# A Fourier-mixing and cosine-gated feed-forward kernel: one batch's transform work three steps later, one table load moved, another PSUM bank for the special offsets

## The chip, the cores and the metric

One NeuronCore of one Trainium2 chip runs the kernel, which works in float32 throughout. The metric is the device time of one execution in microseconds (us), the median of several runs. The profile is of one further execution.

## The reference

```python
X = np.fft.fft(x, axis=1)            # x: (8, 3008, 256)
X = np.fft.fft(X, axis=2)
x = X.real.reshape(24064, 256)
h = x @ w_in                         # (256, 2048)
g = h * np.cos(h)
out = g @ w_out                      # (2048, 256)
```

## The kernel before, in words

**The transform.** The DFT along the last axis is folded into the first weight: `WC` and `WS` are the cosine and sine tables times `w_in`. The DFT along the sequence, 3008 = 47 x 64, is done in two stages for each of the 8 batches. In the first stage rows of x are loaded into tiles `xp` (four for a batch, p = 0 to 3), GpSimd (POOL) folds each of them (`fold_x`, L376), TensorE (PE) multiplies the folded tile by the table `L2` (`pair_half`, L399), ScalarE (ACT) copies the result out of PSUM (`keep_z`, L410), POOL folds it again (`fold_z`, L417), and DMAs write it to a scratch tensor `zd` in DRAM (`store_pair`, L485). `load_z` (L495) reads `zd` back in another layout, one DMA pair for each half of the partitions. In the second stage (`second_half`, L509) PE multiplies that by the table `BJ`, one group g of 6 at a time.

Offsets 0 and 32 of the 64, and column 128, do not fit the folding and are done apart. Their rows of x are loaded into `xz` at the end of `load_xx(b, 0)` (L216), `fold_ends` (L390 on POOL, and a small ACT copy at L287 that waits in the list `small` for the next half step) folds them, `take_middle` (L369) collects column 128 of each `xp`, and once in a batch `middle` (L447) multiplies both into one PSUM tile `pm`. VectorE (DVE) clears `pm` first (`clear_middle`, L433), and ACT copies it to `zm` afterwards (L1067).

**The main part.** A step is one batch, one group g and one of 8 parts fp of the hidden width: 8 x 6 x 8 = 384 steps. Group 0 has T = 225 columns, the others 256. A step has two halves, u = 0 and 1, and the loop over k (L1022) runs through the halves, with t = k // 2 the step. For one half: ACT writes the seed of a PSUM bank (`seed`, L680), PE adds the `WC` product and then the `WS` product (`mm1`, L699), between them ACT copies out twice the first sum (`act_e`, L711), DVE forms the mirrored half of the columns (`dve_h`, L715), ACT rounds (L727), DVE takes the fraction (L731), ACT takes the sine (L737), and DVE multiplies (`dve_g`, L741). POOL forms sums of the four quarters of a step (`sums`, L757, L763, L764), and seven products with w_out and its combinations go into the accumulators `M` (`mm2`, L790), five halves later. Results leave by `take_m`, `combine_m`, a transpose on DVE (`store_out`, L910) and output DMAs (`send_out`, L928).

**Order.** All engines work through their instructions in the order of the program, and the order is written out by hand. The four banks `H0` to `H3` of the halves go round: `psum("H")` takes the next bank, and `borrow(name, k)` takes the bank that the k-th next half will get. Thus `borrow` with k = 0 is the bank of the half that is three halves back, and with k = 1 that of the half two back, which is `old` in the loop and which `dve_g(old)` reads.

While the steps of batch b run, the work of batch b + 1 is done between them. `transform(b)` (L547) makes a table from step number within the batch (0 to 47) to calls; at the end of step t the loop makes the calls that stand under t % 48. Before this table's calls of a step come those of `opening`, a table for the first steps of all. The pair products of tile p run at the start of step 8p + 9 (`pairs`), `middle` runs in the second half of step 10 (`middles`), the loads of `zd` are issued after steps 23 and 39, and `second_half` follows from step 42 on. Nearly all DMAs are issued by the SP queue, in the order of the program.

Batch 0 is transformed ahead of the loop, by other functions (`chunk`, `first_half`). The first batch to which `transform` applies is b = 1, whose work runs during steps 0 to 47. Just ahead of the loop the SP queue issues the rest of the loads, the last of them

```python
load_bj(1024, NJ * 128)
nc.sync.dma_start(out=L2, in_=L2_dr.ap())
```

and during steps 0 to 6 `opening` also has POOL combine parts of w_out (`combine_w2`, L665).

Of the kernel before, what the change touches and what calls it, by code (L numbers as in the profile page):

```python
# [21 lines left out]
NJ = 24  # L22
# [107 lines left out]
def kernel(  # L130
# [113 lines left out]
    def load_bj(c0, c1):  # L244
        nc.sync.dma_start(out=BJ[:, c0:c1], in_=B_dr.ap()[:, c0:c1])
# [4 lines left out]
    def load_w2(f0, f1):  # L250
        nc.sync.dma_start(
            out=w2.rearrange("p (q c) -> p q c", c=ND)[:, 2 * f0 : 2 * f1],
            in_=moe_w_out.rearrange("(q p) c -> p q c", p=128)[:, 2 * f0 : 2 * f1],
        )
# [24 lines left out]
    def borrow(name, k=0):  # L279
        return ppool.tile([128, 512], FP, tag=f"H{(turn[0] + k) % 4}", bufs=1, name=name)  # L280
# [115 lines left out]
    def pair_half(b, p, q, pz):  # L396
        rows = slice(64 * q, 64 * q + 64)
        for h in range(2):
            nc.tensor.matmul(  # L399
                pz[64 * h : 64 * h + 64],  # L400
                lhsT=L2[rows, 0:64],
                rhs=ws[b, p][rows, 512 * h : 512 * h + 512],
                start=True,
                stop=True,
            )
# [23 lines left out]
        small.append(dict(out=zv[:, 1, :, 0].rearrange("y (q s) -> y q s", s=2), in_=zq[:, p]))  # L429

    def clear_middle():
        pm = borrow("pm", 1)[:, 0:144]
        nc.vector.memset(pm, 0.0)  # L433
        return pm

# [100 lines left out]
    def spread_nb(g):  # L536
        pq, nb = ready[0, g]
        T = _width(g)
        pn = borrow("pn") if g else psum("pn", "M")
        nc.tensor.matmul(pn[:, 0:T], lhsT=ones, rhs=pq[0:1, T : 2 * T], start=True, stop=True)  # L540
        nc.scalar.copy(out=nb[:, 0:T], in_=pn[:, 0:T])

    pairs = {}
    middles = set()
    per = NG * 8

    def transform(b):  # L547
        todo = {}

        def at(o, *call):  # L550
            todo.setdefault(o, []).append(call)

        for p in range(4):
            if p < 2:
                at(p, turn_x, b, p)
            at(1 + p, load_xx, b, p)
            at(5 + p, take_middle, b, p)
            for k in range(2):
                at(8 * p + 6 + k, fold_x, b, p, k)
                at(8 * p + 9 + k, fold_z, b, p, k)  # L560
            pairs[per * (b - 1) + 8 * p + 9] = b, p
            at(8 * p + 11, patch_z, b, p)
            at(8 * p + 12, store_pair, b, p)
        for e in range(2):
            at(4 + e, fold_ends, e)
        middles.add(per * (b - 1) + 10)
        at(12, store_ends, b)
        at(23, load_z, b, 0)
        at(39, load_z, b, 1)
        for g in range(NG):  # L570
            at(42 + g, second_half, b, g)
        return todo
# [6 lines left out]
    def weights(e, n, tag="M"):  # L579
        pw = psum("pw", tag)  # L580
        for i in range(2):
            nc.tensor.matmul(
                pw,
                lhsT=CS[i][:, 128 * e : 128 * e + 128],
                rhs=raw(n, i),
                start=(i == 0),
                stop=(i == 1),
            )
        return pw
# [94 lines left out]
    def seed_first(h):  # L684
        s, T = h.s, h.s.T
        nc.tensor.matmul(
            h.H[:, 0:T],
            lhsT=wrow[:, 128 * h.u : 128 * h.u + 128],
            rhs=s.pq[0:1, T : 2 * T],
            start=False,  # L690
            stop=True,
            skip_group_check=True,
        )

    def mm1(h, e):
        s, T = h.s, h.s.T
        W = WS if e else WC
        f = 2 * s.fp + h.u
        nc.tensor.matmul(  # L699
            h.H[:, 0:T],  # L700
            lhsT=W[:, 128 * f : 128 * f + 128],
            rhs=s.pq[:, e * T : e * T + T],
            start=False,
            stop=True,
            skip_group_check=True,
        )

    def act_e(h):
        T = h.s.T
        h.ew = spool.tile([128, 256], FP, tag="ew", bufs=2, name="ew")  # L710
        nc.scalar.mul(out=h.ew[:, 0:T], in_=h.H[:, 0:T], mul=2.0)  # L711
# [11 lines left out]
    def act_round(h):  # L723
        if h.u == 0:
            h.s.r = spool.tile([128, 1024], FP, tag="r", bufs=4, name="r")
        r, y = sides(h)
        nc.scalar.activation(out=r, in_=y, func=AF.Copy, bias=BIG, scale=1.0)  # L727
# [11 lines left out]
    def dve_g(h):  # L739
        r, y = sides(h)  # L740
        nc.vector.scalar_tensor_tensor(  # L741
            out=r, in0=y, scalar=-0.25, in1=r, op0=ALU.add, op1=ALU.mult
        )
# [237 lines left out]
    for half in range(2):  # L981
        load_z(0, half, 4)
    load_w2(4, 6)
    load_w2(6, 8)
    load_bj(1024, NJ * 128)
    nc.sync.dma_start(out=L2, in_=L2_dr.ap())
    opening = {
        0: ((combine_w2, 0, 2), (combine_w2, 2, 4)),
        3: ((combine_w2, 4, 6, 0, 2),),
        4: ((combine_w2, 4, 6, 2, 4), (second_half, 0, 1)),  # L990
        5: ((combine_w2, 6, 8, 0, 2), (spread_nb, 1)),
# [15 lines left out]
    def step(t, last=None):  # L1007
        s = steps[t] if 0 <= t < n else None
        return s if s is not None and (last is None or s.fp == 7) else None
# [3 lines left out]
    def unit(k):  # L1013
        return halves[k] if 0 <= k < 2 * n else None
# [7 lines left out]
    for k in range(2 * n + LAG):  # L1022
        t, u = divmod(k, 2)
        d, v = divmod(k - LAG, 2)
        cur, prev, old, nxt = unit(k), unit(k - 1), unit(k - 2), unit(k + 1)
        done = step(d)
        full = step(d if v else d - 1, True)
        if cur:
            if k % (2 * per) == 0:
                todo = transform(cur.s.b + 1) if cur.s.b + 1 < NB else {}  # L1030
            if k >= AHEAD:
                mm1(cur, 0)
                act_e(cur)
            if k == 0:
                for h in (cur, nxt):
                    mm1(h, 0)
                    seed_first(h)
                    act_e(h)
                spread_nb(0)
            if k < AHEAD - 1:  # L1040
                mm1(cur, 1)
            if k == 0:
                pw = [weights(1, 3)]
        pair = None if u else pairs.pop(t, None)
        if old:
            dve_g(old)
            if old.u:
                sums(old.s)
        pm = clear_middle() if u and t in middles else None
        if done:  # L1050
            order = (0, 1, 5, 4, 3, 2, 6) if done is steps[-1] else range(7)
            mm2(done, 4 * v, 4 * v + (1 if pair else 3), order)
        if pair:
            pz = [borrow("pz"), borrow("pz", 1)]
            for q in range(2):
                pair_half(*pair, q, pz[q])
            mm2(done, 4 * v + 1, 4 * v + 3, order)
        if pm is not None:
            middle(pm)
        if full and full is not steps[-1]:  # L1060
            take_m(full, 1 if v else 3, nc.vector)
        if nxt and 0 < k < AHEAD - 1:
            seed(nxt)
        if prev:
            act_round(prev)
        if pm is not None:
            nc.scalar.copy(out=zm, in_=pm)  # L1067
        if pair:
            keep_z(*pair, 0, pz[0])
        if nxt and k >= AHEAD - 1:  # L1070
            seed(nxt)
        if full and full is not steps[-1]:
            take_m(full, 0 if v else 2, nc.scalar)
        if prev:
            dve_frac(prev)
        if k + 1 in range(2, AHEAD):
            mm1(nxt, 0)
            act_e(nxt)
        if k in (1, 2):
            pw.append(weights(0, 4 - k))  # L1080
        copy_small()
        if prev:
            act_sin(prev)
        if pair:
            keep_z(*pair, 1, pz[1])
        if cur and k >= AHEAD - 1:
            mm1(cur, 1)
        if done and v == 0:
            mm2(done, 3, 4, order)
        if cur:  # L1090
            dve_h(cur)
        if k in (1, 2, 3):
            e, q = ((1, 3), (0, 3), (0, 2))[k - 1]
            keep_weights(e, q, pw[k - 1], nc.vector.tensor_copy)
        if k == 3:
            send_wn(3)
        elif k == 6:
            load_wn(3, nc.scalar)
        if u == 0:
            continue  # L1100
        for i in range(6):
            s = step(t - 4 - i, True)
            if s:
                combine_m(s, i)
        for sg, lag in ((0, 8), (1, 10)):
            s = step(t - lag, True)
            if s:
                store_out(s, sg)
        for call in opening.pop(t, ()):
            call[0](*call[1:])  # L1110
        for call in todo.pop(t % per, ()):
            call[0](*call[1:])
# [31 lines left out]
```

## Time and profile before

| | |
|---|---|
| median of 3 runs | 1943.36 us (1943.05 to 1944.39) |
| profiled execution, its own time | 1944.56 us |
| span of the profile, first to last instruction | 1942.8 us |
| busy: PE, DVE, ACT, POOL | 99%, 75%, 77%, 73% |
| mean granted TensorE clock | 0.997 |
| DMA | 108.67 MB, 56 GB/s over the span |

Times in the profile are counted from its first instruction. PE matmul records come in two passes for each float32 matmul, so x2 in a row is one matmul. The span is short of the execution's own time by 1.8 us, which lie outside the first and last instruction. A row of the timeline gives start, duration, engine, line, operation, tile written and tiles read, shape and count, and in brackets the idle time of that engine before it, with what ended it.

### The profile page before, as it was taken

The numbers are of one execution on the slowest core, as the hardware profiler recorded it, in microseconds if no ns is written. First come the engines' busy times: TensorE is split into PE (matmuls) and PEld (weight loads), VectorE is DVE, ScalarE is ACT, GpSimd is POOL, SyncE is SP. The second block draws the span as 40 slices with busy tenths as digits, with TensorE's granted clock in tenths as the row PEclk, the third lists the DMA queues.
The fourth block names the chain that finished last, engine by engine and source line by source line (L and its number), as shares of the span: only waits on it lengthen the run. The fifth ranks groups of instructions, "written<-read, shape, count | busy, mean of one in ns | idle before, by whom it ended". The sixth has DMA issues, their size and how long they took to land.

```text
span 1942.8 us, 29912 instructions
## 1 busy us (share of the span) xinstructions
PE 1920.9 (99%) x9248; PEld 1680.4 (86%) x9248; DVE 1461.9 (75%) x2532; ACT 1496.0 (77%) x3367; POOL 1422.7 (73%) x1693
## 2 busy tenths in 40 slices
PE   9899999999999999999999999999999999999998
PEld 4788898888988889888898888988889888898887
DVE  3577777777777777777877777777777777788787
ACT  3677777777787777777877787777877787777775
POOL 3677768777677876887768876687867887666775
PEclk9999999999999999999999999999999999999999
DMA  7712026111250112501233111421115111110001
GB/s 202 182 28 47 19 46 143 27 36 24 60 129 22 38 41 55 119 18 42 44 82 86 25 40 42 111 57 38 25 42 140 27 41 28 39 22 16 12 14 31
DMA packets 200144, 108.67 MB, mean 56 GB/s; under 512 B 112801, under 2 KB 184047, under 8 KB 199666
## 3 DMA queue, kind: packets, MB, share of 16 engines
q1 hardware_dynamic: 198284, 106.23, 23.1%
q8 instruction: 75, 1.23, 0.3%
q10 hardware_dynamic: 1702, 0.53, 0.1%
q14 instruction: 83, 0.68, 0.1%
HBM read 69.44 MB, written 48.39 MB: 61 GB/s over the span
## 4 chain that ended last, share of the span: by engine, by line
PE 84%; DMA 6%; SPq 3%; DVE 2%; ACT 2%; POOL 1%; issue 1%; ACTq 0%; DVEq 0%; POOLq 0%
PE M L790 51%; PE H L699 29%; DMA xp<-in_x_dram 3%; PE pb L509 2%; PE pz L399 1%; SPq L209 1%; SPq L928 1%; DVE r L731 1%; ACT r L737 1%; DVE r L741 1%; DMA nb<-nd 1%; DMA xp<-xr 0%; SPq L216 0%; DMA wn<-wd 0%; DVE ob L910 0%
## 5 line engine op out<-in xcount | busy, mean ns | idle before, releaser
L757 POOL TENSOR_TENSOR S<-r 128x512 f32<-128x512 f32 (+1 forms) x383 | 475.5, 1242 | 405.3 <-DVE r L741 352.4
L737 ACT ACTIVATE r<-r 128x512 f32<-128x512 f32 (+1 forms) x768 | 477.0, 621 | 255.2 <-DVE r L731 253.7
L731 DVE SCALAR_TENSOR_TENSOR r<-r,H 128x512 f32<-128x512 f32 (+1 forms) x768 | 518.8, 676 | 196.7 <-ACT r L727 170.4
L741 DVE SCALAR_TENSOR_TENSOR r<-H,r 128x512 f32<-128x512 f32 (+1 forms) x768 | 519.1, 676 | 135.8 <-ACT r L737 95.2
L790 PE MATMUL M<-S,VX 128*128 128x256 f32 (+1 forms) x2304 | 621.1, 377 | 0.0
L790 PEld LDWEIGHTS M<-S,VX 128*128 128x128 f32 x2304 | 436.2, 190 | 72.1 <-issue 22.7
L699 PE MATMUL H<-pq,WS 128*128 128x256 f32 (+1 forms) x1536 | 451.8, 376 | 5.8 <-ACT ew L711 5.8
L699 PE MATMUL H<-pq,WC 128*128 128x256 f32 (+1 forms) x1536 | 453.2, 377 | 0.1
L727 ACT ACTIVATE r<-H 128x512 f32<-128x512 f32 (+1 forms) x768 | 447.9, 583 | 0.2 <-DVE H L715 0.2
L715 DVE TENSOR_TENSOR H<-ew,H 128x256 f32<-128x256 f32 (+1 forms) x768 | 325.0, 423 | 126.0 <-PE H L699 65.7
L790 PE MATMUL M<-r,w 128*128 128x256 f32 (+1 forms) x1536 | 387.8, 375 | 0.0
L680 ACT ACTIVATE H<-nb,wn 128x256 f32<-128x256 f32 (+1 forms) x766 | 366.3, 478 | 0.9
L711 ACT ACTIVATE ew<-H 128x256 f32<-128x256 f32 (+1 forms) x768 | 288.1, 375 | 94.0 <-PE H L699 88.8
L699 PEld LDWEIGHTS H<-pq,WS 128*128 128x128 f32 x1536 | 290.6, 190 | 41.6 <-ACT ew L711 6.3
L790 PEld LDWEIGHTS M<-r,w 128*128 128x128 f32 x1536 | 300.2, 196 | 27.4 <-DVE mr L815 0.4
L699 PEld LDWEIGHTS H<-pq,WC 128*128 128x128 f32 x1536 | 280.5, 190 | 42.8 <-ACT H L680 6.5
L763 POOL TENSOR_TENSOR S<-S,r 128x256 f32<-128x256 f32 (+1 forms) x383 | 275.9, 720 | 30.0
L764 POOL TENSOR_TENSOR S<-r,S 128x256 f32<-128x256 f32 (+1 forms) x383 | 275.3, 719 | 30.0
L790 PE MATMUL M<-S,w 128*128 128x256 f32 (+1 forms) x768 | 225.5, 375 | 0.0
L790 PE MATMUL M<-r,VX 128*128 128x256 f32 (+1 forms) x768 | 225.2, 375 | 0.0
L790 PEld LDWEIGHTS M<-S,w 128*128 128x128 f32 x768 | 150.7, 197 | 14.7
L790 PEld LDWEIGHTS M<-r,VX 128*128 128x128 f32 x768 | 145.8, 190 | 14.6
(88 smaller groups left out, 912.4 us busy)
## 6 DMA issues: line engine op xcount, KB each, us to landing
out_dram<-ob SPq DMA_DIRECT2D x724, 32.0 KB
xp<-in_x_dram SPq DMA_DIRECT2D x119, 128.0 KB
xp<-xr SPq DMA_DIRECT2D x112, 128.0 KB
z<-zd SPq DMA_DIRECT2D x28, 384.0 KB
xr<-in_x_dram SPq DMA_DIRECT2D x14, 752.0 KB
zd<-zs SPq DMA_DIRECT2D x98, 96.0 KB
nb<-nd SPq DMA_DIRECT2D x39, 128.0 KB
wr<-in_moe_w_in_dram SPq DMA_DIRECT2D x8, 256.0 KB
```

Of the source, the lines that this page charges most:

```text
L680: nc.scalar.activation(out=h.H[:, 0:T], in_=s.nb[:, 0:T], func=AF.Copy, bias=0.25, scale=wn[:, f : f + 1])
L699: nc.tensor.matmul(h.H[:, 0:T], lhsT=W[:, 128 * f : 128 * f + 128], rhs=s.pq[:, e * T : e * T + T], start=False, stop=True, skip_group_che ...
L711: nc.scalar.mul(out=h.ew[:, 0:T], in_=h.H[:, 0:T], mul=2.0)
L715: nc.vector.tensor_tensor(out=h.H[:, T : 2 * T][:, ::-1], in0=h.ew[:, 0:T], in1=h.H[:, 0:T], op=ALU.subtract)
L727: nc.scalar.activation(out=r, in_=y, func=AF.Copy, bias=BIG, scale=1.0)
L731: nc.vector.scalar_tensor_tensor(out=r, in0=r, scalar=-BIG, in1=y, op0=ALU.add, op1=ALU.subtract)
L737: nc.scalar.activation(out=r, in_=r, func=AF.Sin, bias=0.0, scale=SIN_SCALE)
L741: nc.vector.scalar_tensor_tensor(out=r, in0=y, scalar=-0.25, in1=r, op0=ALU.add, op1=ALU.mult)
L757: tt(out=sv[:, 0:2], in0=qv[:, 1:2].to_broadcast([128, 2, T]), in1=qv[:, 0:4:3], op=ALU.subtract,)
L763: tt(out=sv[:, 2], in0=sv[:, 1], in1=gv[:, 0, 0], op=ALU.subtract)
L764: tt(out=sv[:, 3], in0=gv[:, 1, 0], in1=sv[:, 2], op=ALU.add)
L790: nc.tensor.matmul(acc[key][m // 2][:, 256 * (m % 2) : 256 * (m % 2) + T], lhsT=w, rhs=a, start=first, stop=s.fp == 7, skip_group_check=True,)
```

## The change

`transform(b)` gets a shift `sh`, which is 3 for batch 1 and 0 for all others. For batch 1 everything from `take_middle` on (folds, pairs, patches, stores) comes three steps later, `fold_ends` six steps later, and the two `load_z` one step later. The loads of x (`turn_x`, `load_xx`) and `second_half` stay where they are. The load of the larger part of `BJ` leaves the place ahead of the loop and is made at the end of step 2. And `clear_middle` takes the bank of the next half to be seeded, in all batches, with the clearing made ahead of `dve_g(old)` and `sums` on DVE and POOL.

```diff
     def clear_middle():
-        pm = borrow("pm", 1)[:, 0:144]
+        pm = borrow("pm")[:, 0:144]
         nc.vector.memset(pm, 0.0)
         return pm
...
+        sh = 3 if b == 1 else 0
         for p in range(4):
             if p < 2:
                 at(p, turn_x, b, p)
             at(1 + p, load_xx, b, p)
-            at(5 + p, take_middle, b, p)
+            at(5 + sh + p, take_middle, b, p)
             for k in range(2):
-                at(8 * p + 6 + k, fold_x, b, p, k)
-                at(8 * p + 9 + k, fold_z, b, p, k)
-            pairs[per * (b - 1) + 8 * p + 9] = b, p
-            at(8 * p + 11, patch_z, b, p)
-            at(8 * p + 12, store_pair, b, p)
+                at(8 * p + sh + 6 + k, fold_x, b, p, k)
+                at(8 * p + sh + 9 + k, fold_z, b, p, k)
+            pairs[per * (b - 1) + 8 * p + sh + 9] = b, p
+            at(8 * p + sh + 11, patch_z, b, p)
+            at(8 * p + sh + 12, store_pair, b, p)
         for e in range(2):
-            at(4 + e, fold_ends, e)
-        middles.add(per * (b - 1) + 10)
-        at(12, store_ends, b)
-        at(23, load_z, b, 0)
-        at(39, load_z, b, 1)
+            at(4 + 2 * sh + e, fold_ends, e)
+        middles.add(per * (b - 1) + sh + 10)
+        at(sh + 12, store_ends, b)
+        at(23 + sh // 2, load_z, b, 0)
+        at(39 + sh // 2, load_z, b, 1)
...
-    load_bj(1024, NJ * 128)
     nc.sync.dma_start(out=L2, in_=L2_dr.ap())
     opening = {
         0: ((combine_w2, 0, 2), (combine_w2, 2, 4)),
+        2: ((load_bj, 1024, NJ * 128),),
...
+        pm = clear_middle() if u and t in middles else None
         if old:
             dve_g(old)
             if old.u:
                 sums(old.s)
-        pm = clear_middle() if u and t in middles else None
```

## The prediction

> **What bounds the kernel now.** I read the page's table of busy times first, then the list of waits: PE's own, then all.
>
> ```profile
> PE 1920.9 (99%) x9248; PEld 1680.4 (86%) x9248; DVE 1461.9 (75%) x2532; ACT 1496.0 (77%) x3367; POOL 1422.7 (73%) x1693
> ...
> PE H L699 <- ACT ew L711: 5.8, 2, 5.2
> PE pm L447 <- DVE pm L433: 3.9, 7, 0.8
> PE pz L399 <- POOL xf L383: 1.5, 1, 1.5
> ...
> POOL xzf L390 <- DMA xz<-in_x_dram: 10.6, 1, 10.6
> ACT xzf L287 <- DMA xz<-in_x_dram: 6.1, 1, 6.1
> ```
>
> PE is the bound: it is busy for 1920.9 of 1942.8 us, so only what keeps PE idle or slow can be won, some 20 us at most. Three rows (total, times, longest) name most of that idle time: one wait of 5.2 us for ACT, one of 1.5 us for POOL, and seven of 0.56 us on average for DVE's clearing of `pm`. The last two rows say that POOL and ACT stood still once, for 10.6 and 6.1 us, for the same load, that of `xz`. The timeline around it, and then the same stretch as windows (busy times of PE, PEld, DVE, ACT, POOL; granted clock; DMA share; GB/s):
>
> ```profile
> 49.48 1.30 SPq L245 DMA_DIRECT2D BJ<-dft_B  x1
> 59.78 0.60 SPq L186 DMA_DIRECT2D xr<-in_x_dram  x1
> 71.53 0.19 ACT L287 COPY xzf<-xz 128x2 f32<-128x2 f32 x1 [6.15 <-DMA xz<-in_x_dram]
> 71.58 0.45 POOL L390 TENSOR_TENSOR xzf<-xz 128x127 f32<-128x127 f32 x1 [10.55 <-DMA xz<-in_x_dram]
> 72.50 1.12 PE L699 MATMUL H<-pq,WS 128*128 128x225 f32 x2 [5.25 <-ACT ew L711]
> ...
> 70.25:72.50 2.25, 0.00 (x0) 0.00 (x0) 0.27 (x1) 0.97 (x4) 0.93 (x2) 0.50 0.49 84
> 72.50:77.08 4.58, 4.58 (x12) 4.11 (x13) 2.63 (x5) 2.88 (x7) 4.27 (x9) 0.50 1.08 310
> 86.80:90.00 3.20, 3.19 (x18) 2.10 (x19) 0.68 (x2) 1.99 (x5) 2.85 (x6) 1.00 0.28 55
> ```
>
> `fold_ends` stands in POOL's and ACT's queues in steps 4 to 6, but `xz` lands only at 71.5 us. ACT, stopped at the small copy, cannot make `ew`, and PE stops until 72.50. When PE resumes, the granted clock is 0.50 for another 4.58 us, so about 2.3 us more go there. The 1.5 us wait at 86.8 us is what POOL is behind by then: the pair of step 9 needs a fold that POOL, 10.55 us late, has not finished. That gap leaves the clock at 1.00.
>
> **The opening: ten microseconds.** I price steps 6 to 13 of batch 0 as a whole, by the starts of the `WC` matmuls, two groups to a step. Step 6 starts at 63.56, step 14 at 112.69. For the clean pace: steps 52 and 56 (four steps of T = 225) and steps 11 and 14 (three of T = 256); then step 17, which holds a pair, and step 18; and one `second_half`, from the chain:
>
> ```profile
> 63.56 0.65 PE L699 MATMUL H<-pq,WC 128*128 128x225 f32 x2
> 112.69 0.59 PE L699 MATMUL H<-pq,WC 128*128 128x256 f32 x2
> ...
> 304.25 0.54 PE L699 MATMUL H<-pq,WC 128*128 128x225 f32 x2
> 320.99 0.59 PE L699 MATMUL H<-pq,WC 128*128 128x256 f32 x2
> ...
> 98.45 0.60 PE L699 MATMUL H<-pq,WC 128*128 128x256 f32 x2
> ...
> 127.83 0.59 PE L699 MATMUL H<-pq,WC 128*128 128x256 f32 x2
> 133.90 0.59 PE L699 MATMUL H<-pq,WC 128*128 128x256 f32 x2
> ...
> 97.72 0.89 PE pb L509 x8
> ```
>
> Before: 112.69 - 63.56 = 49.13 us for eight steps. A clean step takes (320.99 - 304.25) / 4 = 4.19 us at T = 225 and (112.69 - 98.45) / 3 = 4.75 us at T = 256; a pair adds 133.90 - 127.83 - 4.75 = 1.32, a `second_half` 0.89 and `middle` 0.59 (a row below). After: steps 6 and 7 at 4.19, steps 8 and 9, where the widths change, at the mean 4.47, step 10 with its `second_half` 4.75 + 0.89, step 11 4.75, step 12 with the pair that came from step 9 6.07, step 13 with `middle` 4.75 + 0.59. The sum is 39.1 us, a gain of 10.0: the stall 5.25, the slow clock 2.3, POOL's arrears 1.5, a first `pm` wait, and 0.5 of small gaps.
>
> This needs `xz` to be there when its fold comes, at the end of step 10. The new step 10 ends about 63.56 + 2 x 4.19 + 2 x 4.47 + 5.64 = 86.5 us, 15 us after `xz` landed before. The table load no longer stands ahead of x on the SP queue (49.48 against 59.78), so x comes no later up to `xz`; in fact somewhat earlier, which buys nothing more. The load of the 1 MB of `BJ` now follows `xz` and is wanted in step 10; its price is among the rivals.
>
> **The clearing of pm: 4.4 us.** One of the seven, batch 3's, on PE and on DVE:
>
> ```profile
> 570.33 1.03 PE L790 MATMUL M<-r,w 128*128 128x256 f32 x4
> 571.19 0.59 PE L790 MATMUL M<-r,VX 128*128 128x256 f32 x2
> 572.33 0.29 PE L447 MATMUL pm<-xm,L 128*64 128x16 f32 x4 [0.54 <-DVE pm L433]
> ...
> 572.92 0.70 PE L699 MATMUL H<-pq,WS 128*128 128x256 f32 x2
> ...
> 571.21 0.69 DVE L741 SCALAR_TENSOR_TENSOR r<-H,r 128x512 f32<-128x512 f32 x1 [0.35 <-ACT r L737]
> 572.00 0.18 DVE L433 MEMSET pm<- 128x144 f32 x1
> ```
>
> PE waits for the memset, and the memset for `dve_g` ahead of it, whose bank it shares. With the bank of the half three back, which DVE finished a half step earlier, it runs ahead of `dve_g`, in the 0.35 us in which DVE waits for the sine anyway: 0.18 us, hidden. The wait on PE is larger than the bracket: matmuls start every 0.43 us (571.19 - 570.33 for two), so the next could have started at 571.62 and `pm` starts at 572.33, 0.71 us late against 0.54 in the bracket. So six batches (the first is in the sum above) give 3.9 x 6 / 7 + 6 x 0.17 = 4.4 us. ACT reads `pm` before it writes the next seed in either order, so the shared bank adds no wait there. If the memset did have to wait, `dve_g`, then the fraction and `dve_h` of that half stand behind it on DVE, and ACT's sine and PE's next `WS` behind those; I take zero, since the bank's last reader precedes it on DVE itself.
>
> **The moved folds: nothing.** The pairs and copies on PE and ACT are the same number in other steps. On POOL, `fold_z` now meets `combine_m`, most in steps 13, 21, 29 and 37, where L834 is the long one:
>
> ```profile
> 176.83 1.27 POOL L417 TENSOR_TENSOR zs<-zr 128x508 f32<-128x508 f32 x1
> ...
> 196.06 1.27 POOL L834 TENSOR_TENSOR cb<-cb,mr 128x512 f32<-128x512 f32 x1
> ...
> 197.96 1.28 POOL L757 TENSOR_TENSOR S<-r 128x512 f32<-128x512 f32 x1 [0.63 <-DVE r L741]
> ```
>
> A step with L834 leaves POOL 0.63 us idle. Another 1.27 us puts it 0.64 us behind for one step, and the sums are wanted by PE about three half steps after their inputs are made. I take zero, with 0.6 us a time, 2.6 us in all, as the bound.
>
> **The later stores: 1.0 us lost.** The last store to `zd` moves from step 36 to 39, the last `load_z` from 39 to 40, and `second_half` stays at 42. SP issues in order, and step 39 already has eight output stores. SP's rows for the old step 36 and step 39, windows in which the transfers end, and PE at step 42:
>
> ```profile
> 226.07 1.82 SPq L485 DMA_DIRECT2D zd<-zs  x4
> 243.93 4.64 SPq L928 DMA_DIRECT2D out_dram<-ob  x8
> 248.62 1.30 SPq L495 DMA_DIRECT2D z<-zd  x2
> ...
> 229.00:230.00 1.00, 1.00 (x6) 0.90 (x5) 0.69 (x1) 0.67 (x3) 0.84 (x3) 1.00 0.03 8
> ...
> 253.00:254.00 1.00, 1.00 (x6) 0.90 (x5) 1.00 (x3) 0.85 (x3) 0.92 (x2) 1.00 0.76 132
> 254.00:255.00 1.00, 1.00 (x6) 0.88 (x6) 1.00 (x2) 0.90 (x3) 0.41 (x1) 1.00 0.11 24
> ...
> 257.26 1.05 PE L509 MATMUL pb<-BJ,z 128*128 128x128 f32 x8
> ```
>
> In the old times: the stores would be issued behind the output stores, at 248.6. Their data took from 226.07 to about 229.1, at most 3.4 us with the signal; the load took from 248.62 to 253.8, at most 6.2. So the load lands between 248.6 + 3.0 + 5.2 = 256.8 and 248.6 + 3.4 + 6.2 = 258.2, and PE wants it at 257.26: a wait of 0 to 1.0 us, once. I take 1.0, since both the load and PE wait for signals, not for data. The Trainium skill would have it otherwise (DMA: Bandwidth & Descriptors, Anatomy of one DMA: about 2.0 us fixed and the bytes over 436 GB/s, a fit for DMAs issued by GpSimd): by my estimate from it the load of twice 384 KB lands before 257 and the wait is nothing, the total 1929.0 in place of 1930.0. The rows speak against it: these transfers need over 5 us.
>
> **The sum.** 10.0 + 4.4 - 1.0 = 13.4 us off the profiled execution's own 1944.56: 1931.2. That execution lies 1.2 us over the median of the runs, 1943.36, so the median to expect is 1930.0.
>
> **Rivals.** *The table load delays x.* The 1 MB now goes between the first and the second `xp`:
>
> ```profile
> BJ<-dft_B SPq DMA_DIRECT2D x1, 1024.0 KB
> ...
> 55.00:56.00 1.00, 1.00 (x7) 0.94 (x7) 0.93 (x2) 0.66 (x2) 1.00 (x3) 1.00 1.08 411
> ```
>
> At 411 GB/s that is 2.6 us for `xp` 1 to 3, and POOL may stop at `take_middle` in steps 9 to 11, each time for up to that long. For it: DMAs are the busiest resource there. Against: the folds come three steps later too, about 14 us. PE would lose 1 to 3 us: 1931 to 1933. *Half of the opening's stall stays*, because ACT or POOL in steps 4 to 12 meets another late transfer or copy: 5 us of the ten, 1935. Against: the two idle brackets above name `xz` alone. *It does not do what it says*: the opening is short of transfers as such, PE stops at another load just as long, and only `pm` is won, 4.4 - 1.0: 1940. Against: the rows of steps 4 and 5 show no other wait of that size. *Slower*: the stores and the load of step 42 slip further, since `zd` is filled by a chain of POOL, ACT and SP. PE then waits 4.75 us for each step of slip, and after a long gap runs at half clock for 6.8 us or so (70.25 to 77.08), 3.4 us lost. It decides only from a wait of about 15 us, three steps, at which 14.4 are won and 1.0 + 3 x 4.75 + 3.4 = 18.7 lost: 1947.7. Against: SP has nothing to issue between the stores of step 39 and that load. The Trainium skill (TensorE: Matmul & The Clock Gate, The HAM clock gate) puts the halving at an idle window of about 3.4 us; the trace brackets it, 1.5 us without and 5.25 us with it, so by either the 1.0 us wait costs only itself.
>
> **How the numbers follow.** Chances: the forecast 0.72, the table load's delay 0.12, half a stall 0.08, no effect 0.04, slower 0.04. The range runs from 1928.0 (no wait at step 42, and 1 us for the paces' rounding) to 1935.5 (the first two rivals, or POOL's bound of 2.6 with a longer wait at step 42); it leaves out the last two. A measurement of this kernel can tell about 0.2%, 3.9 us, from no change: the forecast and the first two rivals are faster by more (0.92), 1940 is within it (0.04), the last is slower (0.04).
>
> **What would show it.** In the profile after: the waits of ACT L287 and POOL L390 for `xz` gone, no PE gap near 70 us and no 0.50 clock there, `pm` L447 out of PE's waits, step 14 starting near 102.7, and a PE wait of `pb` L509 for the load of `zd` of about 1 us at step 42, near 247 us. Wrong: a new stretch at half clock in the first 110 us, a wait of POOL L369 for `xp` that PE feels, or `pb` waiting several us.

## The result, and the profile after

The changed kernel takes 1930.85 us (median of six runs, 1930.4 to 1932.1) against 1943.84 (six runs) of the kernel before: ratio 0.9933, 95% interval 0.9920 to 0.9946. The prediction was 1930.0, in a range of 1928.0 to 1935.5. The profiled execution took 1931.02 us, against 1944.56. From line 553 on, lines are one higher in the changed kernel, and two higher in some of the experiments.

The page's busy times and PE's own waits (total, times, longest):

```profile
PE 1917.1 (99%) x9248; PEld 1677.5 (87%) x9248; DVE 1462.1 (76%) x2532; ACT 1496.4 (78%) x3367; POOL 1422.2 (74%) x1693
...
PE pb L509 <- DMA z<-zd: 1.8, 1, 1.8
...
PE H L700 <- ACT ew L712: 0.5, 1, 0.5
```

The 5.2 us for ACT, the 1.5 us for POOL and the seven waits for `pm` are gone. One new wait has come, PE's for the load of `zd` of batch 1 (the kernel before waits once for such a load, 0.4 us, ahead of the loop). Steps 6 and 14 by their `WC` matmuls, the late fold of `xz`, and two windows (busy PE, PEld, DVE, ACT, POOL; granted clock; DMA share; GB/s):

```profile
61.23 0.65 PE L700 MATMUL H<-pq,WC 128*128 128x225 f32 x2
100.43 0.68 PE L700 MATMUL H<-pq,WC 128*128 128x256 f32 x2
...
87.46 0.45 POOL L390 TENSOR_TENSOR xzf<-xz 128x127 f32<-128x127 f32 x1
...
60.00:70.00 10.00, 10.00 (x52) 9.23 (x51) 7.32 (x14) 7.53 (x19) 8.46 (x11) 1.00 0.73 216
70.00:80.00 10.00, 10.00 (x52) 9.40 (x51) 7.76 (x14) 8.16 (x20) 6.16 (x10) 1.00 1.06 287
```

Steps 6 to 13 take 100.43 - 61.23 = 39.20 us. No bracket stands behind L390: `xz` had long landed. PE is busy throughout and the clock is 1.00. The clearing and the middle of batch 3, on DVE and PE:

```profile
559.90 0.18 DVE L433 MEMSET pm<- 128x144 f32 x1
560.27 0.69 DVE L742 SCALAR_TENSOR_TENSOR r<-H,r 128x512 f32<-128x512 f32 x1 [0.19 <-ACT r L738]
...
560.26 0.59 PE L791 MATMUL M<-r,VX 128*128 128x256 f32 x2
560.79 0.29 PE L447 MATMUL pm<-xm,L 128*64 128x16 f32 x4
560.93 0.53 PE L447 MATMUL pm<-xzf,L 128*64 128x128 f32 x6
561.39 0.70 PE L700 MATMUL H<-pq,WS 128*128 128x256 f32 x2
562.36 0.68 PE L700 MATMUL H<-pq,WC 128*128 128x256 f32 x2
```

The memset now runs in the time in which DVE waits for the sine, and of that wait 0.19 is left. At step 42 the SP queue issues the stores of tile 3, then the load, and PE waits:

```profile
237.06 1.91 SPq L485 DMA_DIRECT2D zd<-zs  x4
240.69 1.30 SPq L495 DMA_DIRECT2D z<-zd  x2
...
247.14 1.13 PE L509 MATMUL pb<-BJ,z 128*128 128x128 f32 x8 [1.82 <-DMA z<-zd]
```

Where the 13.54 us between the two profiled executions lie, by the starts of the steps: 2.33 ahead of step 2, 9.93 in steps 6 to 13, -0.15 in steps 14 to 41 with the three moved pairs, -2.06 in step 42, and 3.5 in the middles of the other six batches.

### The profile page after: what moved, and what is told of

Same layout as the page of the kernel before. It is cut to its first block, busy times and chain, and to the rows that moved or that the text cites. A ratio compares the mean times of both kernels' runs of the same rounds, so it can differ in the third digit from the quotient of the medians.

```text
span 1929.2 us, 29913 instructions
## 1 busy us (share of the span) xinstructions
PE 1917.1 (99%) x9248; PEld 1677.5 (87%) x9248; DVE 1462.1 (76%) x2532; ACT 1496.4 (78%) x3367; POOL 1422.2 (74%) x1693
## 4 chain that ended last, share of the span: by engine, by line
PE 88%; DMA 4%; SPq 3%; POOL 3%; DVE 1%; ACT 1%; issue 1%; POOLq 0%; DVEq 0%
PE M L791 53%; PE H L700 30%; PE pb L509 2%; PE pz L399 2%; DMA xp<-xr 1%; DMA xp<-in_x_dram 1%; SPq L209 1%; SPq L929 1%; POOL xf L376 1%; POOL S L758 1%; PE pw L583 1%; DMA nb<-nd 0%; POOL S L764 0%; SPq L216 0%; DVE r L742 0%
```

## The experiments

**The clearing alone.**

```diff
-        pm = borrow("pm", 1)[:, 0:144]
+        pm = borrow("pm")[:, 0:144]
 # and the call of clear_middle ahead of dve_g(old)
```

> The kernel before with the change to clear_middle alone (bank of the next seed, cleared ahead of dve_g). Theory, the seven waits of PE for the clearing are a loss of their own: they go, and nothing takes their place, so 3.5 to 4.4 us less than before (1939.5 to 1940.3), the stall near 70 us as before. Rival, the bank shared with the next seed gives the time back (the seed, and PE's next WC product, now wait for pm and its copy): less than 1 us gained, and new waits of PE for ACT's seed once a batch.

Measured: 1941.29 us against 1944.72, ratio 0.9982 (0.9972 to 0.9991), 3.4 us. PE's waits have no row for `pm` any more, and no wait for ACT's seed. The waits went and nothing took their place, as the theory had it; the gain lies just under its 3.5 to 4.4 us, with 1.8 to 5.4 as the interval. The first row of PE's waits did change, though nothing near 70 us was touched; its longest is 7.2 us where it was 5.2 (the kernel before again, below, shows why):

```profile
PE H L699 <- ACT ew L711: 7.7, 2, 7.2
```

**The bank alone.** Only the first of the two edits, the call left where it was.

> The kernel before with the other bank for pm alone, the clearing left behind dve_g. Theory, the place in DVE's order decides: the clearing still runs when dve_g is done, the seven waits of PE stay at 3.9 us, nothing gained (1943 to 1945.5). Rival, the bank alone frees it: the waits go, as with both.

Measured: 1944.77 us (one run). The waits stay, and on DVE the memset still comes after `dve_g`:

```profile
PE pm L447 <- DVE pm L433: 3.4, 7, 0.7
...
571.22 0.69 DVE L741 SCALAR_TENSOR_TENSOR r<-H,r 128x512 f32<-128x512 f32 x1 [0.35 <-ACT r L737]
571.94 0.18 DVE L433 MEMSET pm<- 128x144 f32 x1
```

So the place in DVE's order is what pays. The other bank only allows it, since `dve_g(old)` still reads the old one.

**The table load alone.**

```diff
-    load_bj(1024, NJ * 128)
     nc.sync.dma_start(out=L2, in_=L2_dr.ap())
     opening = {
+        2: ((load_bj, 1024, NJ * 128),),
```

> The kernel before with the table load at step 2 alone. Theory, the stall is the lateness of xz and any microsecond by which x comes earlier shortens it: xz lands some 4 us earlier, PE's wait of 5.25 falls to 1 to 1.5 us, the half clock does not come, so 6 to 8 us less than before (1936 to 1938). Rival, only the shift of the folds matters: xz is bound by something other than the table (the queue waits for an earlier DMA to land), 0 to 1 us gained.

Measured: 1942.22 us, ratio 0.9988 (0.9979 to 0.9998), 2.5 us (interval 0.4 to 4.1): between the two, nearer to the rival. The first row is the SP queue's own wait in the kernel before, the others SP's wait, SP and PE in this one:

```profile
SPq L186 <- DMA wn<-wd: 8.5, 1, 8.5
```

```profile
SPq L191 <- DMA wn<-wd: 5.5, 1, 5.5
...
50.66 0.61 SPq L186 DMA_DIRECT2D xr<-in_x_dram  x1
56.81 0.56 SPq L191 DMA_DIRECT2D xr<-in_x_dram  x1
66.08 1.81 SPq L216 DMA_DIRECT2D xz<-in_x_dram  x4
...
70.40 1.12 PE L699 MATMUL H<-pq,WS 128*128 128x225 f32 x2 [3.78 <-ACT ew L711]
```

Without the table the first copy to `xr` goes at 50.66, but the second still stands until 56.81. By the waits, what SP waits for there is the small `wn` load of the ACT queue (why one queue waits for the other's load, no run here shows), and `xz` is issued at 66.08 where it was 68.32. The table was a part of the lateness only. PE resumes 2.1 us earlier, and still at a clock of 0.50.

**The shift alone.** The changed `transform`, with the table load and the clearing as before.

> The kernel before with the shift of batch 1 alone (table load ahead of x, clearing as before). Theory, once xz is folded six steps later it is there with 15 us to spare, so the table load's place is worth nothing: the whole 10 us of the opening are won and 2 us lost at step 42, 8 us less than before (about 1935.8), no PE wait near 70 us. Rival, x as a whole comes too late without the move: POOL stops at take_middle in steps 8 to 11, PE feels it, and the gain is 5 us or less.

Measured: 1934.97 us, ratio 0.9948 (0.9931 to 0.9964), 9.75 us. PE's waits and step 42:

```profile
PE pm L447 <- DVE pm L433: 3.5, 6, 0.8
...
247.32 0.91 PE L509 MATMUL pb<-BJ,z 128*128 128x128 f32 x6 [1.41 <-DMA z<-zd]
```

No wait near 70 us. Steps 6 to 13 take 39.3 us. With the clearing's 3.4 that makes 13.2 us, the whole change (13.0 between the medians), so these medians leave nothing for the table load. The theory holds; that the gain is 9.75 us and not 8 is taken up under the sum below.

**Only the special offsets later.** `take_middle` and the folds of x stay in their steps.

```diff
-            at(4 + e, fold_ends, e)
-        middles.add(per * (b - 1) + 10)
-        at(12, store_ends, b)
+            at(4 + 2 * sh + e, fold_ends, e)
+        middles.add(per * (b - 1) + sh + 10)
+        at(sh + 12, store_ends, b)
 # patch_z and store_pair of tile 0 also sh = 3 steps later
```

> The kernel before with only the special offsets of batch 1 later (fold_ends at steps 10 and 11, middle at 13, the patch and store of tile 0 and the store of the ends three steps later); take_middle and all folds and pairs of x stay. Theory, it is ACT's wait for xz that stops PE at once: ACT no longer waits, POOL now waits for xp at take_middle in step 5 until about 70 us, and PE feels that only through the sums, 1.5 to 3 us, without a half clock; POOL's arrears at the pair of step 9 stay; 4 to 7 us less than before. Rival, POOL's standstill is as bad as ACT's: PE idle over 3.4 us near 70 us, half clock, at most 2 us gained.

Measured: 1942.77 us, ratio 0.9990 (0.9981 to 0.9999): 2.0 us, the rival's figure. ACT no longer waits for a load there, but POOL does, at the `take_middle` of tiles 0, 1 and 3, and PE at the sums, later than expected and longer (POOL at tile 0 and twice at tile 1, PE, and a window after it):

```profile
68.19 0.20 POOL L369 TENSOR_TENSOR xm<-xp 64x4 f32<-64x4 f32 x1 [1.43 <-DMA xp<-xr]
77.51 0.20 POOL L369 TENSOR_TENSOR xm<-xp 64x4 f32<-64x4 f32 x1 [1.34 <-DMA xp<-xr]
79.90 0.20 POOL L369 TENSOR_TENSOR xm<-xp 64x4 f32<-64x4 f32 x1 [2.20 <-DMA xp<-xr]
...
81.30 1.12 PE L792 MATMUL M<-S,VX 128*128 128x225 f32 x2 [4.42 <-POOL S L759]
...
81.30:87.60 6.30, 6.02 (x18) 3.42 (x19) 0.69 (x1) 2.08 (x5) 5.63 (x10) 0.50 1.06 216
```

The two waits for `xz` in the profile of before were thus only the first of several. With `xz` out of the way, `xp` takes its place. All of x is late, so `take_middle`, which waits for it here, has to move too. The folds of x show no such wait here.

**Half of x copied earlier, no shift.**

```diff
+    turn_x(1, 0)
     load_w2(4, 6)
     load_w2(6, 8)
 # and no call of turn_x(1, 0) at step 0
```

> The kernel before with one thing moved: turn_x(1, 0), the copy of a half of x of batch 1 to the scratch tensor xr, is issued ahead of the loads of parts 4 to 7 of w_out. Theory, xz is late because everything of x stands on the SP queue behind that copy (its issue waits for the wn load to land, and the loads from xr wait for the copy to land, 59.8 to 65.6 us before): with the copy done early xz is issued some 4 to 6 us earlier, PE's wait falls by as much, and 4 to 7 us are won without any shift. Rival, the loads are bound by the DMA engines' rate in that stretch (0.81 to 0.90 busy): another 0.75 MB ahead only pushes back the rest, and at most 1 us is won.

Measured: 1941.43 us, ratio 0.9986 (0.9977 to 0.9996), 3.3 us. The profiled execution took 1940.17:

```profile
63.34 1.92 SPq L216 DMA_DIRECT2D xz<-in_x_dram  x4
...
67.36 0.45 POOL L390 TENSOR_TENSOR xzf<-xz 128x127 f32<-128x127 f32 x1 [5.04 <-DMA xz<-in_x_dram]
68.28 1.12 PE L699 MATMUL H<-pq,WS 128*128 128x225 f32 x2 [3.40 <-ACT ew L711]
```

`xz` is issued 5.0 us earlier and lands 4.2 earlier, and PE resumes 4.2 earlier. Of that 3.3 is seen in the median (interval 0.8 to 4.5), short of the theory's 4 to 7; the median alone would not quite rule out the rival's 1, but the rows do: the order on the SP queue set the end of the stall. After the 3.40 us that are left of the stall the clock is still 0.50.

**The kernel before again.**

> The kernel before, unchanged, for a second profile. In the first one the clock was granted at 0.50 from 36 to 39.5 us and step 0 took 6.96 us; in all later kernels step 0 takes 5.26. Theory, that is the chance of one execution and the stall near 70 us swallows it, since it ends when xz lands: step 0 at 5.26, PE idle about 7 us in place of 5.25, and PE resuming at 72 to 73 us as before. Rival, it belongs to the kernel before: step 0 at 6.96 again.

Measured: 1944.72 us against 1944.75. Step 0 takes 5.26 us at a clock of 1.00, and PE resumes at the old time after a longer wait:

```profile
72.53 0.74 PE L699 MATMUL H<-pq,WS 128*128 128x225 f32 x1 [6.17 <-ACT ew L711]
```

The four kernels with the old opening, and four with the shift:

| kernel | step 6 starts | PE resumes | step 14 starts | steps 6 to 13 |
|---|---|---|---|---|
| before | 63.56 | 72.50 | 112.69 | 49.13 |
| before again | 62.67 | 72.53 | 112.66 | 49.99 |
| bank alone | 61.99 | 72.63 | 112.75 | 50.76 |
| clearing alone | 61.79 | 72.66 | 112.27 | 50.48 |
| changed | 61.23 | - | 100.43 | 39.20 |
| changed, again | 62.24 | - | 101.44 | 39.20 |
| shift alone | 61.82 | - | 101.09 | 39.27 |
| tile 0 alone, again | 62.78 | - | 101.98 | 39.20 |

In the old opening PE resumes at 72.5 to 72.7 whenever it stops, since a landing ends the wait: what an execution wins before it, the wait takes back. With the shift it is kept. So steps 6 to 13 are worth 9.9 us from the first profile, 10.8 from the second, and up to 11.6 from the others.

**The later load of zd, later still.**

```diff
-        at(39 + sh // 2, load_z, b, 1)
+        at(39 + 2 * (sh // 2), load_z, b, 1)
```

> The changed kernel with the second load of zd of batch 1 another step later, at 41 in place of 40, behind the eight output stores of step 41. Theory, the wait of PE at step 42 is this load's landing in the order of the SP queue: the load is issued about 6 to 7 us later, so the wait grows from 1.8 to about 8 us, passes the limit of the clock, and with the half clock 8 to 10 us are lost against the changed kernel (1939 to 1941). Rival, the load is not what ends the wait (the stores of zd, or the copies, are): the wait grows by 2 us or less.

Measured: 1937.43 us (one run), 6.6 us over the changed kernel, less than expected. SP, PE and two windows:

```profile
241.14 4.61 SPq L929 DMA_DIRECT2D out_dram<-ob  x8
245.79 1.29 SPq L495 DMA_DIRECT2D z<-zd  x2
...
252.16 1.19 PE L509 MATMUL pb<-BJ,z 128*128 128x128 f32 x4 [7.02 <-DMA z<-zd]
...
248.40:252.16 3.76, 0.00 (x0) 0.03 (x1) 0.00 (x0) 0.00 (x0) 0.00 (x0) 0.50 0.75 140
252.16:255.24 3.08, 3.08 (x11) 2.85 (x12) 0.00 (x0) 0.84 (x3) 0.00 (x0) 0.50 0.00 0
```

The load is issued 5.1 us later, PE waits 5.2 us longer: one is the other, and the rival is out. The half clock was priced too high. It lasts 6.8 us, but PE is still idle for 3.76 of them, so only 3.08 us of work run slowly, 1.5 us lost.

**Only tile 0 shifted.** Tiles 1 to 3 are folded and stored as before, both loads at 23 and 39, the rest as in the changed kernel.

```diff
+            so = 0 if p else sh
             for k in range(2):
-                at(8 * p + sh + 6 + k, fold_x, b, p, k)
+                at(8 * p + so + 6 + k, fold_x, b, p, k)
 # so in place of sh in fold_z, pairs, patch_z and store_pair too
```

> The changed kernel with only tile 0 of batch 1 (and fold_ends, take_middle, middle) shifted; tiles 1 to 3 folded, paired and stored as before the change, both loads of zd at steps 23 and 39. Theory, the 2 us at step 42 are the late store of tile 3: PE waits for nothing there and the time is 2 us under the changed kernel (1928.8). Rival, the wait at step 42 only moves (POOL, with tile 1 six steps after tile 0, becomes late and PE waits for a fold at step 17): no gain over the changed kernel, 1930.5 to 1932.

Measured: 1929.76 us, ratio to before 0.9921 (0.9906 to 0.9936). To compare it with the changed kernel on one chip, both were run again:

> The changed kernel again, beside the two that follow on one chip. Theory: 1930 to 1932, the wait of PE at step 42 of 1.8 us as in its first profile, step 0 at 5.26 us.

> The kernel with only tile 0 shifted again, for a comparison with the changed kernel on the same chip. Theory: 2 us under the changed kernel, no PE wait at step 42. Rival: the two are within 0.5 us, the earlier difference being one of chips.

Measured: changed kernel 1931.57 us (1930.82 to 1931.8), tile 0 alone 1930.31 (1929.84 to 1931.37), five runs each. In the latter the stores are issued 22.8 us before the load, and PE goes to `pb` without a wait:

```profile
215.43 1.82 SPq L485 DMA_DIRECT2D zd<-zs  x4
238.24 1.29 SPq L495 DMA_DIRECT2D z<-zd  x2
...
246.62 1.05 PE L509 MATMUL pb<-BJ,z 128*128 128x128 f32 x8
```

Step 42 takes 5.64 us, against 7.29 in the changed kernel beside it. By the medians the gain is 1.1 and 1.3 us, by the step 1.65 to 2.06; 2 us were expected. The step shows that the wait is gone. That the whole kernel is a little faster is likely and not clear of noise: the intervals against the kernel before overlap, and in the four profiles of the two kernels the start of step 6 alone differs by 1.55 us (61.23 to 62.78), which is as much.

**Tile 0 shifted, table load ahead of the loop.**

> The kernel with only tile 0 shifted, but the table load where it was before the change, ahead of the loop. Theory, with the folds late the place of the table load is worth nothing: the same time as the kernel with only tile 0 shifted, within 0.5 us, and no PE wait near 70 us. Rival, the earlier x is needed after all (POOL stops at take_middle in steps 8 to 11): 1 to 3 us longer.

Measured: 1929.8 us beside 1930.31, within the noise. Here SP issues `xz` as late as in the kernel before, and no engine waits for `xz` or `xp`:

```profile
49.24 1.13 SPq L245 DMA_DIRECT2D BJ<-dft_B  x1
67.99 1.81 SPq L216 DMA_DIRECT2D xz<-in_x_dram  x4
```

Steps 6 to 13 take 39.2 us as well. The table's place is worth nothing once the folds are late.

## Why the prediction was right, and where its terms were off

**The opening** was priced at 10.0 us, 39.1 us left for steps 6 to 13. Measured 39.20 to 39.27 left in every kernel with the shift, 9.93 won against the profiled execution. The mechanism holds as far as it went: ACT and POOL stand still for a late load, PE stops, the clock halves. Its reading was too narrow in one place. I argued from the two brackets that `xz` alone was late, and the kernel in which only its fold moved won 2.0 us: `xp` is late too, and `take_middle` had to move with it (whether tile 0's folds had to was not tried alone). The change does move them, so the sum was not touched. That is luck in part: the rival of half a stall, another late transfer, was argued against with those same brackets, and its condition was there. It did not come, nor did no effect: PE is busy throughout from 60 to 80 us. Step 14 started at 100.43 where 102.7 was foretold; the difference lies ahead of step 2 and is told under the sum.

**The table load** was priced at nothing, and as a rival at 1 to 3 us lost. It is nothing, by the kernel with tile 0 shifted and the table load ahead of the loop: SP does wait 2.5 us for that transfer in the changed kernel, among the `xp` loads, but the folds come later than that. The reason I gave was half of the story, for alone it brought 2.5 us.

**The clearing of pm** was priced at 4.4 us for six batches, and measured 3.5. The step that failed is the 0.17 us a time that I added to the bracket. I reckoned from the matmuls ahead of `pm`, which start every 0.43 us. But `pm` starts 0.53 after the last of them even when nothing is waited for (560.26 and 560.79), and the next `WC` product takes about 0.09 us longer (0.68 at 562.36, against 0.59 at 573.89 before). What goes is the bracket, 0.53 us in five batches, and 0.77 in one.

**The moved folds** were priced at nothing, with 2.6 us as the bound: 0.15 us in all.

**The wait at step 42** was priced at 1.0 us, as the upper end of 0 to 1.0, and measured 2.06. The step was right, issue order and two transfers, and the kernel with the load a step later confirms it. The size was off by its smaller parts. In the old times, 12.1 us later than the new ones at step 42, the stores were issued 0.55 us later than the 248.6 I took. From them to the load it took 3.63 us, where I took at most 3.4. From the load to PE's start it took 6.45 us, where I took at most 6.2. Together that is the missing 1.0 us. The estimate from the Trainium skill (DMA: Bandwidth & Descriptors, Anatomy of one DMA), no wait and 1929.0, was the worse one: from issue to PE's start the load took those 247.14 - 240.69 = 6.45 us, where by my estimate that rule gives under 4.

**The sum** came out by luck: these errors, 0.9 and 1.06 us too hopeful, met one of the other sign. The profiled execution of before had an unlucky opening, 2.33 us longer by step 2 than that of the changed kernel. In the kernel before such a loss disappears in the stall, in the changed one it does not. So the sum from one profile missed gain. By the eight profiles of the table step 14 starts 11.4 us earlier with the shift on average, where I counted 10.0 for steps 6 to 13. With that, and with a step 42 that loses 1.65 us in other profiles where it lost 2.06 in the first, the 11.2 us by parts become about the 13.0 between the medians. By the parts alone the forecast would have been near 1932.

**Slower** did not come. Its price was too high: the half clock after a long wait cost 1.5 us where I took 3.4, since PE stands still in part of it. It is no fixed price either: after the other gaps PE worked for 3.0 to 6.0 us at 0.50, and half of that is lost.

## What to carry to other kernels

The wait that ended with a landing DMA was fixed here in its end, not in its length: it swallowed the gains ahead of it, and when it went, those gains came back. So measure what lies before such a stall in more than one profile. The first late load in a list of waits hid those behind it on the same queue; look at what each reader would wait for once the first wait is gone. When work is moved later, look for the last link of its chain, here a store and a load in one queue's order, and move only what had to move: shifting the folds and the store of one tile in place of four avoided the new wait.

## What the runs showed of the hardware

Two of the fourteen profiles, those of the kernel before and of the one with only the special offsets moved, show a granted clock of 0.50 from about 36 to 39.5 us though no PE gap there is over 0.5 us; step 0 then takes 6.95 us in place of 5.26. What decides it stays open. Its window in the kernel before, and the same one in the kernel before again (clock in the third place from the end):

```profile
36.10:39.50 3.40, 3.40 (x6) 1.32 (x5) 1.02 (x2) 0.92 (x2) 3.10 (x5) 0.50 0.62 138
36.10:39.50 3.40, 3.40 (x13) 2.20 (x12) 1.39 (x4) 1.68 (x4) 2.20 (x4) 1.00 0.52 113
```

Apart from that, the clock halved in the loop in each of the eight PE gaps of 3.40 to 7.18 us, and after gaps of up to 1.82 us it did not, which agrees with the idle window of about 3.4 us that the Trainium skill gives (TensorE: Matmul & The Clock Gate, The HAM clock gate) as far as the length of the gaps goes. The moment of the halving does not follow from it: it lay between 2.2 us (in the gap of 3.78) and 3.9 us (in the gap of 4.42) after PE stopped.
